# Steps and transfers of the first third of a fused attention and feed-forward kernel in another order

## The chip, the core and the metric

The kernel runs on one core of a Trainium2 chip. The metric is the device time of one launch in microseconds. Below, PE is TensorE, DVE is VectorE, ACT is ScalarE, POOL is GpSimd and SP is SyncE, which here issues nearly all transfers.

## What is computed

A gated linear attention over 768 positions (4 batches, 8 heads, head width 48) whose output, with the heads side by side, goes through a feed-forward block of width 2048 on 3072 tokens:

```python
def _attn_ref(q, k, v, f_logit) -> np.ndarray:
    B, H, S, D = q.shape
    f = 1.0 / (1.0 + np.exp(-f_logit))
    state = np.zeros((B, H, D, D), dtype=np.float32)
    y = np.zeros_like(q)
    for t in range(S):
        state = f[:, :, t, :, None] * state + np.einsum('bhd,bhe->bhde', k[:, :, t], v[:, :, t])
        y[:, :, t] = np.einsum('bhd,bhde->bhe', q[:, :, t], state)
    return y.astype(np.float32)
...
def _moe_ref(x, w_in, w_out) -> np.ndarray:
    h = x @ w_in
    relu6 = np.clip(h + 3.0, 0.0, 6.0)
    g = h * relu6 / 6.0
    return (g @ w_out).astype(np.float32)
```

## The kernel before

The 768 positions are cut into 6 chunks of 128. A chunk of one batch is a unit, so there are 24 units; unit i belongs to chunk i // 4. The four units of a chunk give one group of 512 tokens for the feed-forward block. The hidden width is cut into 16 blocks of 128, so a group has 16 block steps, and a step is numbered 16 * group + block.

What a unit i does, with the engine and the line of its instruction:

- `load` L371 (the gate logits, SP), `loadq` L378 (q and k, 512 KB, SP), `loadv` L383 (v, SP).
- `gate` L388 (sigmoid, ACT), `back` L395 and `fwd` L419 (the running products of the gates backward and forward, scans on DVE), `rend` L411 and `end` L414, `kmul` L408 and `qmul` L424 (k and q times these products, on DVE or POOL), `decay` L427.
- `tk` L482 (k turned, PE) and `ktok` L489 (its copy, ACT), `kv` L501 (k times v, PE), `carry0` and `carry1` L514 to L523 (the state), `att` L463 (q times k, PE), `mask` L470 (DVE), `qs` L533 and `av` L550 (the two parts of the output, PE).
- `xh` L569, `ym` L573 and `xl` L580 or L582 split the output into a high and a low part for the feed-forward block; `hole` L588 are two transfers of 48 KB that fill the rows which heads of 48 leave open.

What is done to each of the 16 weight blocks, once: `ld` L280 (its 64-bit form, 768 KB, SP), `lim` L290 or L292, `z` L298, `mid` L305, `dif` L310, `top` L314 (it is made a float again on ACT and DVE), `high` L326 (ACT) and `low`, `lowi`, `lowo` L329 (high and low part, DVE or POOL), for blocks 0 to 2 also `wd` L333 (a transfer).

What a block step does: `mm1` L619 (9 matmuls of 512 columns), `relu` L629 (ACT), `g` L633 (DVE), `gh` L642 (ACT), `gl` L646 (DVE or POOL), `mm2` L669 (9 matmuls). Blocks 0 to 2 of the first group are done in halves of 256 tokens, first the two units that come first (`mm1a` L691, `relua` L700, `ga` L705, `mm2a` L710), then the other two (`mm1b`, `relub`, `gb`, `mm2b`, on the same lines). `warm` L1007 and `tiny` L1014 are matmuls on a blank tile, of 512 and of 32 columns, whose results nobody reads.

Nothing schedules this on the chip. A list of 1518 words, ORDER, names every step once, as `step.number`, with the PSUM banks to use as a third part. The loop over ORDER writes the steps out in this order, and each engine works off its own instructions in the order in which they were written:

```python
            if ins.engine in ordered:
                after(ins, ordered[ins.engine])
```

Between engines there are semaphores for true dependencies and for buffers that are used again. All transfers of SP stand in one row, so that one which waits for its buffer holds those behind it. q and k have three buffers in turn, v three, the gates and their products two, PSUM two pairs of banks (0 and 1, 2 and 3) and a single one (4). Which steps run on POOL and on ACT is set by two more lists.

Of the kernel before, what the change touches and what calls it, by code (L numbers as in the profile page):

```python
# [60 lines left out]
mask.2 xl.1 ktok.2 rend.3 kmul.3 dif.1 lim.2 hole.1 wd.0 loadv.4 tk.3.0 fwd.3 kv.2.3 ktok.3 carry0.2 mid.2 z.2 kv.3.0
qmul.3 load.5 qs.2.2 top.1 carry1.3 end.3 carry1.2 att.3.0 dif.2 av.2 high.1 wd.1 ld.3 loadq.5 lowi.0 mm1a.0.4
carry0.3 top.2 gate.4 xh.2 mask.3 high.2 ym.2 qs.3.0 lowi.1 back.4 relua.0 xl.2 av.3 hole.2 mm1a.1.3 xh.3 lowi.2 end.4
ga.0 xl.3 mm2a.0 rend.4 relua.1 gate.5 lim.3 hole.3 ld.4 kmul.4 fwd.4 z.3 mm1a.2.0 ga.1 decay.4 qmul.4 back.5 mid.3
ld.5 tk.4.4 wd.2 mm2a.1 dif.3 ktok.4 ld.6 loadq.6 top.3 load.6 att.4.2 ld.7 kv.4.2 loadv.5 relua.2 ga.2 mask.4
carry0.4 carry1.4 high.3 low.3 lim.4 mid.4 ld.8 mm1b.0.4 ld.9 ld.14 mm1b.2.1 relub.0 z.4 dif.4 ld.10 end.5 loadv.7
lim.5 mm1b.1.0 rend.5 gb.0 relub.1 kmul.5 decay.5 mm1.3.2 top.4 mm2b.0 gb.1 high.4 mid.5 dif.5 z.5 low.4 mm2a.2 lim.6
top.5 mm2b.1 relub.2 mid.6 z.6 fwd.5 mm1.4.4 relu.3 dif.6 high.5 gb.2 g.3 gate.6 qs.4.0 qmul.5 low.5 tk.5.2 av.4
back.6 ktok.5 mm2b.2 loadv.6 xh.4 load.7 top.6 loadq.7 end.6 relu.4 ld.11 kv.5.2 ld.15 g.4 att.5.2 high.6 xl.4 mm1.5.4
gh.3 kmul.6 lim.7 lim.8 low.6 gh.4 gl.3 mm2.3 relu.5 rend.6 carry0.5 z.7 mask.5 carry1.5 z.8 gl.4 mid.7 mm2.4 g.5  # L70
decay.6 dif.7 gh.5 top.7 z.9 mm1.6.4 mid.8 high.7 gl.5 lim.9 dif.8 low.7 mm1.7.3 relu.6 top.8 mid.9 high.8 fwd.6
qs.5.0 relu.7 tk.6.2 av.5 dif.9 lim.10 g.7 mm2.5 loadv.8 xh.5 ld.13 g.6 hole.4 ktok.6 qmul.6 low.8 z.10 mm1.8.4 top.9
ld.12 gate.7 loadq.8 gh.6 back.7 high.9 att.6.2 gh.7 mid.10 gl.6 kv.6.0 lim.11 rend.7 mm2.6 xl.5 z.11 mask.6 kmul.7
dif.10 low.9 tk.7.2 mm1.9.3 ktok.7 top.10 relu.8 fwd.7 high.10 end.7 relu.9 gl.7 mm2.7 g.8 carry0.6 gh.8 g.9 low.10
mm1.10.4 carry1.6 gh.9 qmul.7 lim.12 mid.11 load.9 gl.8 mm2.8 z.12 hole.5 decay.7 dif.11 mid.12 dif.12 qs.6.2 top.11
att.7.0 loadq.9 av.6 load.8 top.12 kv.7.0 high.11 relu.10 gl.9 mm2.9 xh.6 carry0.7 mask.7 z.14 g.10 qs.7.0 xl.6 av.7
low.11 lim.13 z.13 hole.6 mm1.11.2 mid.13 lim.14 xh.7 loadv.9 gh.10 dif.13 high.12 mid.14 gl.10 mm2.10 relu.11 top.13
gate.8 g.11 low.12 mm1.12.3 gh.11 high.13 carry1.7 xl.7 gl.11 mm2.11 hole.7 relu.12 low.13 z.15 dif.14 loadq.10 gate.9
top.14 mm1.13.4 back.8 high.14 low.14 mm1.14.1 relu.13 g.13 g.12 gh.13 mm1.16.0 kmul.8 lim.15 gl.13 mid.15 dif.15
tk.8.2 top.15 mm2.13 back.9 high.15 end.8 gh.12 low.15 mm1.15.4 relu.14 rend.8 gl.12 fwd.8 mm2.12 relu.15 relu.16  # L80
qmul.8 ktok.8 g.14 load.10 att.8.2 g.15 gh.14 kv.8.2 g.16 mm1.17.4 mask.8 rend.9 gl.14 fwd.9 mm2.14 gate.10 gh.15
qmul.9 gl.15 mm2.15 lowo.0 back.10 mm1.19.1 outs.0 outv.1 end.9 gh.16 outs.2 kmul.9 gl.16 relu.17 mm1.18.0 od.2
load.11 rend.10 relu.19 g.17 od.0 decay.8 carry0.8 fwd.10 mm2.16 relu.18 g.19 end.10 carry1.8 g.18 tk.9.3 qmul.10
load.12 mm1.20.4 loadv.10 ktok.9 od.1 gh.17 kmul.10 lowo.1 gh.18 gate.11 decay.9 gl.17 qs.8.0 att.9.2 loadq.11 av.8
kv.9.2 xh.8 carry0.9 mm2.17 gate.12 carry1.9 mask.9 decay.10 lowo.2 back.11 mm1.21.2 gl.18 end.11 gh.19 gl.19 xl.8
tk.10.3 relu.21 mm2.18 ktok.10 g.21 relu.20 rend.11 back.12 qs.9.0 gh.21 fwd.11 att.10.2 loadq.12 av.9 kv.10.0 qmul.11
mm2.19 g.20 load.13 loadv.11 carry0.10 gl.21 loadv.12 carry1.10 rend.12 mm1.22.4 fwd.12 mask.10 mm2.21 relu.22 g.22
kmul.12 decay.11 gh.22 kmul.11 mm1.23.3 gate.13 qmul.12 xh.9 back.13 load.14 hole.8 relu.23 gl.22 mm2.22 xl.9 g.23
hole.9 tk.11.4 qs.10.0 ktok.11 att.11.2 gh.20 loadq.13 av.10 gate.14 gl.20 kv.11.0 loadv.13 tk.12.4 rend.13 mm2.20
ktok.12 gh.23 end.12 gl.23 mask.11 mm1.24.4 decay.12 kmul.13 mm1.25.3 mm2.23 relu.25 relu.24 g.25 g.24 mm1.29.3 gh.24  # L90
gl.24 fwd.13 mm1.26.4 relu.29 gh.25 xh.10 qmul.13 gl.25 mm2.25 load.15 xl.10 relu.26 carry0.11 back.14 mm2.24 g.29
g.26 qs.11.0 gh.26 att.12.2 gl.26 av.11 kv.12.2 xh.11 loadv.14 mm2.26 hole.10 gh.29 carry1.11 mask.12 gate.15
carry0.12 loadq.14 carry1.12 rend.14 mm1.27.4 tk.13.2 relu.27 mm1.30.3 g.27 gl.29 xl.11 mm2.29 relu.30 hole.11 gh.27
g.30 end.13 kmul.14 mm1.28.1 gl.27 gh.30 ktok.13 gl.30 decay.13 back.15 tk.14.0 mm2.30 fwd.14 mm1.31.2 qmul.14 load.16
mm1.32.4 relu.31 relu.28 g.31 end.14 g.28 mm2.27 relu.32 ktok.14 qs.12.0 gh.28 att.13.2 gh.31 loadq.15 gl.28 av.12
g.32 kv.13.2 xh.12 mm2.28 decay.14 gate.16 mask.13 rend.15 carry0.13 carry1.13 fwd.15 mm1.33.4 xl.12 qs.13.2 qmul.15
gl.31 load.17 att.14.0 loadv.15 av.13 kv.14.0 xh.13 mm2.31 relu.33 xl.13 kmul.15 back.16 hole.13 tk.15.2 g.33 end.16
loadq.16 mm1.35.3 ktok.15 hole.12 carry0.14 outv.4 gh.32 end.15 outs.3 gl.32 loadv.16 gate.17 rend.16 mm1.36.2 gh.33
decay.15 fwd.16 outs.5 relu.35 mm2.32 g.35 carry1.14 qmul.16 gl.33 load.18 mm1.34.4 kmul.16 gh.35 back.17 mm2.33
# [1058 lines left out]
```

## Time and profile before

| | |
|---|---|
| median of 3 runs | 460.57 us (460.49 to 461.0) |
| span of the profiled execution, first to last instruction | 458.9 us |
| PE busy | 448.2 us, 98% |
| DVE busy | 329.8 us, 72% |
| ACT busy | 225.9 us, 49% |
| POOL busy | 95.0 us, 21% |
| transfers | 44.95 MB, 98 GB/s over the span |

The profiled execution has no time of its own beside its span. The median of the runs is 1.7 us more than the span; this lies before the first and after the last instruction. A busy share is a mean over stages: in the first 110 us DVE is as busy as PE, and the transfers are busy in the first 60 us alone. Times inside the trace are counted from the first instruction.

### The profile page before, as it was taken

The page shows a single profiled execution, that of the slowest core. Times are in us where ns is not written, and L with a number is a line of the kernel's source. Part 1 is how long each engine was busy: PE and PEld are TensorE (multiplying, and loading weights), DVE is VectorE, ACT ScalarE, POOL GpSimd, SP SyncE. Part 2 cuts the span into 40 slices and gives each one's busy share as a digit, 9 for nine tenths or more (in the row PEclk, how much of TensorE's full clock was granted, in tenths as well). Part 3 has the DMA queues.
Part 4 walks back from the last instruction along what each step waited for, and adds up shares of the span by engine and source line. Part 5 has one row for each costly group of instructions (what it writes and reads, how often), then busy time and mean ns, then how long its engine had stood idle before and what let it go on. Part 6 is the DMA issues. An engine that isn't in the chain of part 4 may idle for free.

```text
span 458.9 us, 11919 instructions
## 1 busy us (share of the span) xinstructions
PE 448.2 (98%) x5092; PEld 387.8 (85%) x5092; DVE 329.8 (72%) x538; ACT 225.9 (49%) x390; POOL 95.0 (21%) x110
## 2 busy tenths in 40 slices
...
PEclk9999999999999999999999999999999999999999
...
GB/s 308 270 273 367 413 213 150 99 54 25 182 107 107 23 82 72 123 93 110 84 1 0 102 71 142 62 60 1 70 75 14 14 1 1 23 49 0 1 1 75
DMA packets 19116, 44.95 MB, mean 98 GB/s; under 512 B 2544, under 2 KB 8816, under 8 KB 19056
## 3 DMA queue, kind: packets, MB, share of 16 engines
...
q8 instruction: 42, 0.69, 0.6%
...
q14 instruction: 18, 0.15, 0.1%
...
## 4 chain that ended last, share of the span: by engine, by line
PE 90%; DMA 3%; DVE 3%; issue 1%; ACT 1%; SPq 1%; DVEq 0%; ACTq 0%
PE o L669 33%; PE pair L619 28%; PE single L619 11%; DMA raw<-w 3%; PE pair L533 3%; PE o L833 3%; PE pair L550 2%; PE pair L463 2%; PE single L833 2%; PE pair L833 2%; PE pair L501 2%; PE pair L482 1%; ACT workings L290 0%; DVE workings L314 0%; PE single L482 0%
## 5 line engine op out<-in xcount | busy, mean ns | idle before, releaser
L669 PE MATMUL o<-gg,weight 128*128 128x512 f32 x633 | 148.7, 382 | 0.3 <-issue 0.3
L619 PE MATMUL pair<-xts,weight 128*128 128x512 f32 x594 | 137.6, 381 | 0.0
L669 PEld LDWEIGHTS o<-gg,weight 128*128 128x128 f32 x633 | 117.6, 189 | 16.5 <-issue 0.2
L619 PEld LDWEIGHTS pair<-xts,weight 128*128 128x128 f32 x594 | 110.6, 189 | 15.5 <-DVE tg L633 0.3
L646 DVE TENSOR_TENSOR gg<-tg,gg 128x512 fp32r<-128x512 f32 x76 | 56.2, 746 | 34.4 <-ACT gg L642 34.0
L633 DVE SCALAR_TENSOR_TENSOR tg<-tg,pair 128x512 f32<-128x512 f32 x66 | 44.9, 682 | 41.3 <-ACT tg L629 40.9
L629 ACT ACTIVATE tg<-pair,half 128x512 f32<-128x512 f32 x66 | 44.9, 684 | 59.4 <-PE pair L619 56.7
L642 ACT ACTIVATE gg<-tg 128x512 fp32r<-128x512 f32 x79 | 48.8, 626 | 48.6 <-PE o L669 37.8
L619 PE MATMUL single<-xts,weight 128*128 128x512 f32 x243 | 57.9, 383 | 0.0
L619 PEld LDWEIGHTS single<-xts,weight 128*128 128x128 f32 x243 | 45.2, 189 | 6.6 <-ACT weight L326 0.3
L629 ACT ACTIVATE tg<-single,half 128x512 f32<-128x512 f32 x27 | 18.5, 686 | 31.0 <-PE single L619 28.8
L395 DVE TENSOR_TENSOR_SCAN scans<-scans,ones 112x516 f32<-112x516 f32 (+1 forms) x25 | 30.6, 1229 | 3.8 <-ACT scans L388 3.6
L408 POOL TENSOR_TENSOR qkf<-qkf,scans 112x512 f32<-112x512 f32 x14 | 20.4, 1455 | 59.2 <-DMA qkf<-unit 34.5
L424 POOL TENSOR_TENSOR qkf<-qkf,scans 112x512 f32<-112x512 f32 x11 | 15.8, 1439 | 70.4 <-DVE scans L419 48.7
L419 DVE TENSOR_TENSOR_SCAN scans<-scans,ones 112x516 f32<-112x516 f32 x24 | 29.8, 1240 | 0.4
L569 ACT ACTIVATE xts<-pair 112x512 fp32r<-112x512 f32 x24 | 14.3, 597 | 26.9 <-PE pair L550 22.7
L427 POOL TENSOR_TENSOR carried<-states,ends 112x192 f32<-112x192 f32 x12 | 9.0, 754 | 81.7 <-PE pair L533 48.1
L633 DVE SCALAR_TENSOR_TENSOR tg<-tg,single 128x512 f32<-128x512 f32 x27 | 18.4, 681 | 9.4 <-ACT tg L629 9.4
L470 DVE TENSOR_TENSOR a<-pair,causal 128x512 f32<-128x512 f32 x24 | 16.4, 681 | 8.1 <-PE pair L501 5.3
L582 DVE TENSOR_TENSOR xts<-pair,xts 112x512 fp32r<-112x512 f32 x22 | 15.0, 681 | 8.9 <-ACT xts L569 8.9
L757 POOL TENSOR_TENSOR temporary<-weight 128x256 f32<-128x256 f32 x14 | 10.7, 786 | 44.0 <-DVE tg L633 44.0
L800 ACT ACTIVATE ts<-ts 128x512 fp32r<-128x512 f32 x24 | 14.8, 627 | 9.9 <-DVE ts L796 8.6
...
## 6 DMA issues: line engine op xcount, KB each, us to landing
...
xts<-xts SPq DMA_DIRECT2D x48, 48.0 KB, 2.4
...
```

The source lines that it names most:

```text
L395: nc.vector.tensor_tensor_scan(flat(sf[:, p])[:, ::-1], gt[:, columns(p)][:, ::-1], flat(unit[:, p])[:, ::-1], 0.0, op0=ALU.mult, op1=ALU.add,
L408: engine("kmul", i).tensor_tensor(parts_of(t, 1), parts_of(t, 1), split(sf[:, :, 1:C + 1]), op=ALU.mult)
L419: nc.vector.tensor_tensor_scan(past, past, flat(rend), 0.0, op0=ALU.mult, op1=ALU.add)
L424: engine("qmul", i).tensor_tensor(parts_of(t, 0), parts_of(t, 0), split(to), op=ALU.mult)
L470: nc.vector.tensor_tensor(d["a"].rearrange("r p e t -> r e p t"), d["at"], causal.unsqueeze(1).unsqueeze(1).broadcast_to([128, 2, NP, HC]) ...
L619: nc.tensor.matmul(h, win(f, a, k), turned(g["xt"][:, k, :g["n"] // C, b]), start=i == 0, stop=i == 3 * KT - 1,)
L629: nc.scalar.activation(d["t"], d["h"], AF.Relu, bias=half, scale=1.0 / 6.0)
L633: nc.vector.scalar_tensor_tensor(d["t"], d["t"], 1.0, d["h"], op0=ALU.min, op1=ALU.mult)
L642: nc.scalar.activation(d["gg"][:, 0], d["t"], AF.Copy)
L646: engine("gl", g["first"] + f).tensor_tensor(d["gg"][:, 1], d["t"], d["gg"][:, 0].bitcast(F32), op=ALU.subtract)
L669: nc.tensor.matmul(g["o"][m], wout(f, a, m), halves_of(g[f]["gg"][:, b]), start=i == 0 and first_in(g, m), stop=f == NF - 1 and i == 2, sk ...
L833: nc.tensor.matmul(place[:, part * 256:(part + 1) * 256], left(a), halves_of(right(b)), start=i == 0 and first_in(g, bank_of), stop=False, ...
```

## The change

The first 718 of the 1518 words of ORDER, up to about block step 36 of 96 and unit 16 of 24, stand in another order. They are the same words, with the same banks; nothing else in the file differs, and the rest of ORDER is the same. The first two lines of the table, before and now:

```diff
-load.0 warm.2 loadq.0 warm.7 tiny.60 load.1 loadv.0 loadv.1 loadq.1 ld.0 gate.0 ld.1 back.0 rend.0 kmul.0 gate.1 fwd.0
-end.0 tk.0.2 tiny.12.3 qmul.0 ktok.0 back.1 load.2 kv.0.0 loadq.2 att.0.0 rend.1 warm.2 warm.1 mask.0 lim.0 kmul.1
...
+load.0 warm.2 warm.7 tiny.60 gate.0 warm.2 loadq.0 load.1 loadv.0 back.0 rend.0 kmul.0 loadq.1 ld.0 gate.1 tiny.12.3
+fwd.0 ld.1 loadv.1 tk.0.2 ktok.0 back.1 kv.0.0 carry1.0 qmul.0 rend.1 end.0 load.2 loadq.2 warm.1 carry0.0 fwd.1
```

The transfers that SP issues from the load of unit 3's gates on, before. `raw` is a weight block's 64-bit form (`ld`), `xts` a pair of `hole` transfers, `weight<-workings` is `wd`:

```order
L371 DMA scans_76<-unit 128x517
L378 DMA qkf3_311<-unit 128x1024
L280 DMA raw2_331<-w 128x3072
L588 DMA xts_105<-xts_105 16x3x256 x2
L383 DMA v2_410<-unit 128x400
L383 DMA v3_412<-unit 128x400
L371 DMA scans_76<-unit 128x517
L378 DMA qkf4_450<-unit 128x1024
L588 DMA xts_105<-xts_105 16x3x256 x2
L333 DMA weight0_392<-workings_106 128x384
```

The same place now:

```order
L371 DMA scans_76<-unit 128x517
L280 DMA raw2_285<-w 128x3072
L378 DMA qkf3_336<-unit 128x1024
L280 DMA raw3_361<-w 128x3072
L383 DMA v2_385<-unit 128x400
L383 DMA v3_411<-unit 128x400
L588 DMA xts_105<-xts_105 16x3x256 x2
L371 DMA scans_76<-unit 128x517
L378 DMA qkf4_460<-unit 128x1024
L333 DMA weight0_359<-workings_106 128x384
L588 DMA xts_105<-xts_105 16x3x256 x2
```

Block 2 stands one place ahead of unit 3's q and k, block 3 has come up from a place behind unit 5's gates to one ahead of both `hole` pairs, and `wd.0` stands ahead of the second pair. Further on `ld.4` has come ahead of the pairs of units 2 and 3.

DVE around block 3's `dif` and unit 5's `back`, before: `qmul.4`, `back.5`, `mid.3`, `dif.3`, `top.3`, `ga.2`.

```order
L424 TENSOR_TENSOR qkf4_450<-qkf4_450,scans_76 112x512
L395 SCALAR_TENSOR_TENSOR scans_76<-scans_76,ones_77 112x516
L305 TENSOR_SCALAR workings_106<-workings_106 128x768
L310 TENSOR_TENSOR workings_106<-workings_106 128x768
L314 SCALAR_TENSOR_TENSOR workings_106<-workings_106 128x768
L705 SCALAR_TENSOR_TENSOR th0_2_737<-th0_2_737,pair0_73 128x256
```

The same place now: `mid.3`, `qmul.4`, `decay.4`, `dif.3`, `back.5`, `top.3`, `mask.4`.

```order
L305 TENSOR_SCALAR workings_106<-workings_106 128x768
L424 TENSOR_TENSOR qkf4_460<-qkf4_460,scans_76 112x512
L427 TENSOR_TENSOR carried_97<-states_102,ends_104 112x4x48
L310 TENSOR_TENSOR workings_106<-workings_106 128x768
L395 SCALAR_TENSOR_TENSOR scans_76<-scans_76,ones_77 112x516
L314 SCALAR_TENSOR_TENSOR workings_106<-workings_106 128x768
L470 TENSOR_TENSOR a4_735<-pair1_74,causal_87 128x2x4x64
```

`dif.3` is now ahead of `back.5`; POOL's `kmul.5` waits for `back.5`.

DVE up to `g.3`, before: `top.5`, `mid.6`, `fwd.5`, `dif.6`, `gb.2`, `g.3`.

```order
L314 SCALAR_TENSOR_TENSOR workings_106<-workings_106 128x768
L305 TENSOR_SCALAR workings_106<-workings_106 128x768
L419 SCALAR_TENSOR_TENSOR scans_76<-scans_76,ones_77 112x516
L310 TENSOR_TENSOR workings_106<-workings_106 128x768
L705 SCALAR_TENSOR_TENSOR th1_2_826<-th1_2_826,pair0_73 128x256
L633 SCALAR_TENSOR_TENSOR tg0_3_840<-tg0_3_840,pair1_74 128x512
```

The same place now: `top.5`, `fwd.5`, `low.4`, `mid.6`, `gb.2`, `g.3`, `dif.6`.

```order
L314 SCALAR_TENSOR_TENSOR workings_106<-workings_106 128x768
L419 SCALAR_TENSOR_TENSOR scans_76<-scans_76,ones_77 112x516
L329 TENSOR_TENSOR weight4_823<-workings_106,weight4_823 128x768
L305 TENSOR_SCALAR workings_106<-workings_106 128x768
L705 SCALAR_TENSOR_TENSOR th1_2_821<-th1_2_821,pair0_73 128x256
L633 SCALAR_TENSOR_TENSOR tg0_3_841<-tg0_3_841,pair1_74 128x512
L310 TENSOR_TENSOR workings_106<-workings_106 128x768
```

`dif.6` has gone behind `g.3`; `low.4` stood ahead of `top.5` and is now behind `fwd.5`. On PE `tk.5`, which writes the banks that `g.3` reads, is the first of the steps behind `mm1.4` now; `qs.4`, which waits for `gb.2`, was first before.

## Rows read from the trace of the kernel before

**Rows 1.** The page: clock granted to PE in 40 slices, tenths of full speed.

```profile
PEclk9999999999999999999999999999999999999999
```

**Rows 2.** Windows: stretch, length, busy us of each engine (instructions), clock, DMA share, GB/s.

```profile
13.00:17.00 4.00, 3.54 (x104) 2.29 (x102) 3.70 (x6) 3.26 (x8) 0.00 (x0) 1.00 0.58 168
17.00:27.00 10.00, 8.61 (x306) 6.46 (x305) 9.38 (x16) 8.13 (x18) 1.19 (x1) 1.00 0.85 292
32.00:36.00 4.00, 3.98 (x55) 3.33 (x53) 3.96 (x7) 2.65 (x5) 0.63 (x1) 1.00 0.56 141
36.00:50.00 14.00, 13.53 (x137) 11.37 (x141) 13.26 (x23) 10.94 (x16) 3.19 (x3) 1.00 1.02 405
50.00:110.00 60.00, 59.91 (x721) 50.93 (x722) 58.56 (x94) 45.30 (x65) 16.91 (x11) 1.00 0.43 153
110.00:400.00 290.00, 289.62 (x3193) 253.36 (x3192) 185.64 (x298) 119.92 (x218) 60.70 (x69) 1.00 0.20 63
```

**Rows 3.** Chain that ended last, 31 to 50 us: start, us, what.

```profile
33.46 5.93 DMA raw<-w
...
48.75 0.65 PE pair L533 x28
```

**Rows 4.** Timeline of PE: start, us, instruction, count, idle before it.

```profile
30.09 1.27 PE L691 MATMUL pair<-xts,weight 128*128 128x256 f32 x9
31.20 1.46 PE L710 MATMUL o<-th,weight 128*128 128x256 f32 x6
...
49.39 0.57 PE L482 MATMUL pair<-ident,qkf 112*128 112x112 f32 x4
...
60.84 2.11 PE L619 MATMUL pair<-xts,weight 128*128 128x512 f32 x9
```

**Rows 5.** Timeline of DVE, the same columns.

```profile
10.69 1.42 DVE L419 TENSOR_TENSOR_SCAN scans<-scans,ones 112x516 f32<-112x516 f32 x1
...
21.55 0.69 DVE L470 TENSOR_TENSOR a<-pair,causal 128x512 f32<-128x512 f32 x1 [0.49 <-PE pair L463]
...
28.04 0.69 DVE L470 TENSOR_TENSOR a<-pair,causal 128x512 f32<-128x512 f32 x1
...
35.52 1.45 DVE L310 TENSOR_TENSOR workings<-workings 128x768 int16<-128x768 uint16 x1
...
43.44 0.42 DVE L705 SCALAR_TENSOR_TENSOR th<-th,pair 128x256 f32<-128x256 f32 x1 [0.33 <-ACT th L700]
...
47.82 0.54 DVE L310 TENSOR_TENSOR workings<-workings 128x768 int16<-128x768 uint16 x1
48.27 0.42 DVE L705 SCALAR_TENSOR_TENSOR th<-th,pair 128x256 f32<-128x256 f32 x1
48.60 0.69 DVE L633 SCALAR_TENSOR_TENSOR tg<-tg,pair 128x512 f32<-128x512 f32 x1
...
60.66 0.96 DVE L329 TENSOR_TENSOR weight<-workings,weight 128x768 fp32r<-128x768 f32 x1
```

**Rows 6.** Timeline of POOL, the same columns.

```profile
9.82 1.19 POOL L408 TENSOR_TENSOR qkf<-qkf,scans 112x512 f32<-112x512 f32 x1 [6.78 <-DMA qkf<-unit]
...
35.37 1.18 POOL L408 TENSOR_TENSOR qkf<-qkf,scans 112x512 f32<-112x512 f32 x1 [3.79 <-DVE scans L395]
...
121.82 1.00 POOL L329 TENSOR_TENSOR weight<-weight 128x384 fp32r<-128x384 f32 x1
```

**Rows 7.** Timeline of SP's issues.

```profile
14.95 0.33 SPq L378 DMA_DIRECT2D qkf<-unit  x1
15.33 0.42 SPq L280 DMA_DIRECT2D raw<-w  x1
...
22.86 1.20 SPq L588 DMA_DIRECT2D xts<-xts  x2
```

**Rows 8.** DMA issues, 22.8 to 24.1 us: count, KB each, median us to landing.

```profile
xts<-xts SPq DMA_DIRECT2D x2, 48.0 KB, 3.9
```

**Rows 9.** Timeline of PE's weight loads at 27 us.

```profile
27.24 0.41 PEld L691 LDWEIGHTS single<-xts,weight 128*128 128x128 f32 x3 [0.33 <-DMA xts<-xts]
```

More of the change, by code (lines that the diff above doesn't have):

```diff
@@ L55 @@
 ORDER = """
-load.0 warm.2 loadq.0 warm.7 tiny.60 load.1 loadv.0 loadv.1 loadq.1 ld.0 gate.0 ld.1 back.0 rend.0 kmul.0 gate.1 fwd.0
-end.0 tk.0.2 tiny.12.3 qmul.0 ktok.0 back.1 load.2 kv.0.0 loadq.2 att.0.0 rend.1 warm.2 warm.1 mask.0 lim.0 kmul.1
-fwd.1 tk.1.4 warm.2 z.0 warm.9 qmul.1 ktok.1 mid.0 load.3 carry1.0 dif.0 carry0.0 gate.2 top.0 qs.0.1 end.1 loadq.3
-av.0 back.2 ld.2 warm.1 xh.0 kv.1.3 lim.1 rend.2 fwd.2 ym.0 att.1.2 warm.5 end.2 xl.0 carry1.1 kmul.2 hole.0 carry0.1
-high.0 qmul.2 tk.2.4 qs.1.1 gate.3 mask.1 loadv.2 loadv.3 mid.1 av.1 back.3 att.2.2 load.4 loadq.4 xh.1 warm.3 z.1
@@ L61 @@
[L61 to L99, printed above, removed]
+load.0 warm.2 warm.7 tiny.60 gate.0 warm.2 loadq.0 load.1 loadv.0 back.0 rend.0 kmul.0 loadq.1 ld.0 gate.1 tiny.12.3
@@ new lines @@
+fwd.0 ld.1 loadv.1 tk.0.2 ktok.0 back.1 kv.0.0 carry1.0 qmul.0 rend.1 end.0 load.2 loadq.2 warm.1 carry0.0 fwd.1
+att.0.0 qmul.1 z.0 lim.0 mask.0 warm.2 kmul.1 mid.0 dif.0 load.3 ld.2 warm.9 tk.1.4 warm.1 ktok.1 kv.1.3 gate.2 qs.0.1
+loadq.3 top.0 carry0.1 lim.1 av.0 xh.0 high.0 ld.3 end.1 att.1.2 back.2 ym.0 rend.2 gate.3 loadv.2 carry1.1 warm.5
+kmul.2 fwd.2 tk.2.4 mask.1 xl.0 qs.1.1 qmul.2 loadv.3 hole.0 att.2.2 back.3 lim.2 mid.1 load.4 av.1 z.1 xh.1 mask.2
+xl.1 warm.3 loadq.4 kmul.3 rend.3 dif.1 wd.0 fwd.3 ktok.2 mid.2 tk.3.0 end.2 hole.1 kv.2.3 ktok.3 kv.3.0 loadv.4
@@ new lines @@
+qmul.3 carry0.2 qs.2.2 load.5 top.1 z.2 dif.2 gate.4 end.3 loadq.5 lowi.0 av.2 xh.2 high.1 att.3.0 ym.2 carry1.2 wd.1
+mm1a.0.4 carry0.3 top.2 mask.3 high.2 qs.3.0 av.3 back.4 xl.2 lowi.2 lowi.1 mm1a.1.3 ld.4 hole.2 relua.0 ga.0 kmul.4
+mm2a.0 xh.3 end.4 rend.4 xl.3 lim.3 relua.1 fwd.4 ga.1 tk.4.4 gate.5 z.3 mid.3 mm1a.2.0 hole.3 wd.2 qmul.4 ld.5
+decay.4 dif.3 ld.6 back.5 kmul.5 z.4 top.3 ktok.4 load.6 mm2a.1 att.4.2 carry1.3 kv.4.2 loadv.5 mask.4 carry0.4
+relua.2 ld.7 lim.4 ga.2 mid.4 loadq.6 carry1.4 ld.8 ld.14 high.3 dif.4 ld.10 mm1b.0.4 end.5 relub.0 low.3 mm1b.2.1
```

33 lines of the change are left out of this document (added).

## The prediction, made before the changed kernel was run

> **What bounds the kernel now.** I read the windows first, then the chain, then the timelines of PE, DVE and POOL. The windows [rows 2] split the span. From 50 us on PE is busy 59.91 of 60 us and then 289.62 of 290: whatever the change does, everything behind 50 us is a fixed row of PE work, and the time can fall only by as much as this row starts earlier and isn't interrupted. Ahead of it PE has idle time (0.46 us of 4 in 13 to 17, 1.39 of 10 in 17 to 27, 0.47 of 14 in 36 to 50), and more that is hidden in late matmuls. DVE is the other half: 9.38 of 10 us, 13.26 of 14, 58.56 of 60. Up to 110 us two engines are full, and one order has to please both. The transfers are full from 36 to 50 (share 1.02), yet have holes before: 0.58 in 13 to 17, 0.56 in 32 to 36 [rows 2]. The chain [rows 3] tells what set PE's pace: a weight block took 5.93 us from its issue at 33.46, then work goes over ACT and DVE to PE's `qs.4` at 48.75, which had waited for `gb.2` (48.27 to 48.69 on DVE). Right behind it `tk.5` at 49.39 [rows 4] starts 0.10 after `g.3` ends (48.60 + 0.69 = 49.29) [rows 5]. So PE's last wait ahead of its full stretch is for `g.3` on DVE, and I cost the change on DVE's list up to `g.3`, then on the list up to `low.7`, which PE needs next with little to spare: `low.7` ends at 61.62 [rows 5], and `mm1.7` (from 60.84 [rows 4]) needs it for its last third, near 62.1: 0.5 us. The clock is full in all slices [rows 1]; no gap of PE before cost it a slice, and the number of blank matmuls stays.
>
> **The change part by part.** No step is added or removed, so the work of each engine is the same; only waits move.
>
> *1. DVE, head.* `back.1` stands ahead of `qmul.0` now. It can't start before 8.07 (it waits for unit 1's sigmoid, not moved), so DVE idles some 0.7 us that `qmul.0` filled before; in return the 0.56 us wait of `mask.0` goes. But POOL's `kmul.1` (9.82, 1.19 us [rows 6]) will run behind `qmul.0`, until about 11.1, and `fwd.1` comes just then. The row for this is in the trace: `fwd.1` at 10.69 took 1.42 us [rows 5] and ended 1.10 after `kmul.1` (11.01), the same scan else takes 1.23. So `fwd.1` ends near 12.2, `qmul.1` 12.8, `mask.0` 13.4: weight block 0 (`mid.0`, 12.75 before) starts 0.6 later. From there to `mask.3` DVE took 15.3 us (to 28.04 [rows 5]). In it lie a 0.49 us wait for `att.2` [rows 5], which is ahead of `av.1` on PE now, 0.14 for unit 3's sigmoid, which ACT now does earlier, and hops of 0.1 where a step stands right behind the one it needs, four or five fewer now: 1.05 less. `mask.3` starts near 27.6, 0.45 earlier.
>
> *2. `dif.3`.* It took 1.45 us at 35.52 [rows 5]; the other fifteen take 0.53 to 0.56, as `dif.6` does (0.54). It ended 0.41 after POOL's `kmul.5` (35.37 + 1.18 = 36.55 [rows 6]). DVE stood still behind POOL for 0.9 us. Now `dif.3` stands ahead of `back.5`, and `kmul.5` waits for `back.5`: it can't be hit. `kmul.5` runs beside `top.3` and `mask.4` instead; `mask` reads PSUM, and a mask beside a `kmul` (10.08, beside 9.82) took its usual 0.69. Gain 0.9, cover for POOL 1.5 us against its 1.2.
>
> [...]
>
> *3. DVE from `mask.3` to the end of `g.3`.* Before: 28.04 to 49.29, 21.25 us. The steps at the pitch from start to start that each kind shows when nothing holds it: 4 scans of 1.14, 3 `top` of 0.92, 2 `low` of 0.87 and `lowi.2` 0.45, 3 `dif` of 0.48, 4 `mid` of 0.27, 6 `ga`/`gb` of 0.33, 5 of 0.60 (`qmul`, `mask`, `xl`, `g`), 3 of 0.27 (`decay`, `carry`), 2 `rend` of 0.1: 18.0 us. `dif.6` makes 0.5 more; the rest, 2.75, is waits: 0.98 `dif.3`, 0.33 for `relub.1` [rows 5], 0.2 a scan behind `lowi.1`, some 1.2 in hops and small waits for ACT. `dif.6` stands behind `g.3` now. So `g.3` ends at 27.6 + 18.0 + waits. The waits are 1.77 if all but `dif.3`'s stay and 0 at best; I take 0.6, nearer to the low end, since the steps that followed right behind what they need (`rend.4`/`fwd.4`, `mid.3`/`dif.3`, the two `carry`) now have others between, and since weight blocks 3 to 6 land well ahead (part 4), which frees ACT from its waits. `g.3` ends at 46.2, 3.1 earlier. PE can be there: from `mm1a.0` (27.27) to `tk.5` (49.39) its list is 18.0 us at its own pitch (nine matmuls of 256 columns 1.11, from 30.09 to 31.20 [rows 4]), so 45.3, if `mm1a.0` doesn't come later.
>
> *4. Transfers.* `ld.2` was issued at 15.33, behind `loadq.3` at 14.95, which waits for `qs.0` [rows 7]. It stands ahead now and fills the hole at 13 to 17. `ld.3` (768 KB) and `wd.0` (192 KB) now stand ahead of the second `hole` pair, for which PE waits at 27.24 [rows 9] (issued from 22.86, 3.9 us to landing [rows 7, 8]). At 405 GB/s [rows 2] the 960 KB are 2.4 us; the idle share before was 0.42 x 4 + 0.15 x 10 = 3.2 us. The pair lands between 24.4 and 29.6; with most of the holes filled and the pair issued some 0.5 earlier I take 27.0, no change for PE. `ld.4`, on the chain before, no longer waits for the pairs of units 2 and 3.
>
> *5. What is late next.* Up to `low.7` DVE has the same steps as before, so `dif.6` is paid after all: 3.1 - 0.5 = 2.6 earlier at `low.7`, and PE waits for it. Behind it the lists stay as tight as before. `lowo.2` (1.00 us on POOL [rows 6]) is moved from 122 us, where DVE had time, to behind `low.11`, near 84, beside two `dif`; up to 1.0. PE's blocks of small matmuls change places too. I take 0.4 for all that.
>
> **The sum.** 3.1 - 0.5 - 0.4 = 2.2. Span 458.9 - 2.2 = 456.7, and 1.7 outside the span to the median: 458.4.
>
> **The rivals.** *Same.* All waits of part 3 but `dif.3`'s stay (1.77, not 0.6: 1.2 less), and a step stands still behind `lowo.2` (1.0 instead of 0.4 within it, 0.6 more): 0.4 is left, 460.2. For it: two full engines, where a wait removed is soon found elsewhere. Against: DVE's waits before are few and known by row, and 0.9 of them can't come back at that place. [...]
>
> *More.* No wait on DVE in part 3, none new later, and PE takes up its 0.5 us before `low.7`: 2.2 + 0.6 + 0.4 = 3.2, or 457.4.
>
> *Slower.* The holes of the transfers aren't filled, and the second `hole` pair lands at 29.6. `mm1a.0` then starts 2.4 late, and PE needs 18.0 us and the waits it had (22.1 - 18.0 = 4.1, less 1.0 for `dif.3`): `tk.5` at 50.7 instead of 49.4, so 1.3 slower, 461.9. It decides from a landing later than 28.3. For it: a pair took 3.9 us to land behind less than is ahead of it now. Against: SP stood for `loadq.3` while the transfers idled.
>
> *The change does nothing* needs the same order on the engines; the lists differ from unit 0 on, so no chance of its own.
>
> **How the numbers follow.** Forecast (457.7 to 459.6) 0.52, more 0.13, same 0.23, slower 0.12. Faster by over 0.2% (0.9 us, about what can be told from no change) 0.65, within 0.23, slower 0.12. The range goes from 457.2, below the case with more, to 460.7, past the same; it leaves out the slower case and part of the ends.
>
> **What would show it.** `dif.3` at 0.55 us; `g.3` ending at 46 to 47 and `tk.5` right behind it; the second `hole` pair landing by 28 and the DMA share of 13 to 17 above 0.8; `mm1.7` 2 us or more earlier; PE 99.8% busy from then to 110. Wrong would be: a landing after 28.3, `dif` or scans of over 1.4 us at new places, or PE idle of 0.5 us and more between 50 and 110.

## The result, and the profile after

| | before | after |
|---|---|---|
| median | 460.53 us (459.16 to 461.0, 4 runs) | 465.47 us (463.46 to 466.59, 4 runs) |
| span of the profiled execution | 458.9 us | 464.9 us |

The ratio is 1.0108, 95% interval 1.008 to 1.0136: the new order is 5 us slower, where 2.2 us faster was forecast, and it lies outside the range. Run a second time beside later experiments it took 465.12 us, ratio 1.0099 (1.007 to 1.0127).

The front went much as forecast. The windows of after, columns as in [rows 2]: the hole of the transfers at 13 to 17 is filled (share 0.99, before 0.58). From 50 us on, where PE could lose nothing before, 1.95 us of 60 are idle, and 3.25 of 290. The last two lines are new stretches.

```profile
13.00:17.00 4.00, 3.13 (x135) 2.42 (x134) 3.31 (x6) 3.27 (x6) 0.00 (x0) 1.00 0.99 340
36.00:50.00 14.00, 13.89 (x167) 12.19 (x170) 13.07 (x25) 10.97 (x19) 4.57 (x4) 1.00 1.02 411
50.00:110.00 60.00, 58.05 (x667) 48.12 (x658) 58.79 (x90) 43.15 (x62) 18.65 (x12) 1.00 0.38 133
110.00:400.00 290.00, 286.75 (x3160) 249.48 (x3159) 181.81 (x291) 116.49 (x212) 53.40 (x61) 0.99 0.21 64
62.00:92.00 30.00, 28.05 (x422) 22.73 (x422) 29.77 (x47) 22.71 (x33) 9.33 (x6) 1.00 0.26 81
192.00:196.00 4.00, 4.00 (x15) 3.21 (x14) 2.60 (x6) 0.39 (x2) 0.00 (x0) 0.58 0.27 55
```

The page's clock line, 40 slices of the span. One isn't full, that of 186 to 198 us; before, all were [rows 1].

```profile
PEclk9999999999999999899999999999999999999999
```

PE's timeline of after, columns as in [rows 4]. `tk.5` comes 2.45 us earlier than in [rows 4], `mm1.7` 2.33 earlier (58.51, 60.84). Then three losses show. `mm1.11` waits 0.78 at 85.19, and by `mm1.12` (89.48, before 89.32) the lead is gone. `mm2.22` waits 0.81 for ACT. And in the middle of `av.13`, PE stands still 2.09 us with nothing that it waits for ("issue"); `mm2.31` behind it takes 3.71 us instead of 2.1, at a granted clock of 0.58 over 192 to 196 (last line of the windows), 0.50 over 191.94 to 195.35.

```profile
46.94 0.57 PE L482 MATMUL pair<-ident,qkf 112*128 112x112 f32 x4
...
58.51 0.70 PE L619 MATMUL pair<-xts,weight 128*128 128x512 f32 x2
...
85.19 2.18 PE L619 MATMUL pair<-xts,weight 128*128 128x512 f32 x9 [0.78 <-ACT xts L569]
...
89.48 2.11 PE L619 MATMUL pair<-xts,weight 128*128 128x512 f32 x9
...
140.04 1.13 PE L669 MATMUL o<-gg,weight 128*128 128x512 f32 x4 [0.81 <-ACT gg L642]
...
188.46 0.51 PE L550 MATMUL pair<-a,v 64*48 64x64 f32 x22
191.05 0.42 PE L550 MATMUL pair<-a,v 64*48 64x64 f32 x10 [2.09 <-issue]
191.40 3.71 PE L669 MATMUL o<-gg,weight 128*128 128x512 f32 x9
```

DVE's timeline of after, columns as in [rows 5]: `fwd.1`, `mask.3`, `dif.3`, `g.3`, then between 62 and 92 us `mid.9`, `dif.10`, `mid.11` and `lim.13`. `dif.3` takes 0.55 (before 1.45), and `g.3` ends at 46.83 (before 49.29). But `mid.11` takes 1.45 us, where a `mid` takes 0.35 (67.65).

```profile
9.06 2.01 DVE L419 TENSOR_TENSOR_SCAN scans<-scans,ones 112x516 f32<-112x516 f32 x1
...
27.59 0.69 DVE L470 TENSOR_TENSOR a<-pair,causal 128x512 f32<-128x512 f32 x1 [0.21 <-ACT carried L514]
...
33.56 0.55 DVE L310 TENSOR_TENSOR workings<-workings 128x768 int16<-128x768 uint16 x1
...
46.15 0.68 DVE L633 SCALAR_TENSOR_TENSOR tg<-tg,pair 128x512 f32<-128x512 f32 x1
...
63.12 0.76 DVE L305 TENSOR_SCALAR workings<-workings 128x768 uint16<-128x768 uint16 x1
...
67.65 0.35 DVE L305 TENSOR_SCALAR workings<-workings 128x768 uint16<-128x768 uint16 x1
67.92 0.68 DVE L470 TENSOR_TENSOR a<-pair,causal 128x512 f32<-128x512 f32 x1
68.52 0.95 DVE L310 TENSOR_TENSOR workings<-workings 128x768 int16<-128x768 uint16 x1
...
73.59 1.45 DVE L305 TENSOR_SCALAR workings<-workings 128x768 uint16<-128x768 uint16 x1
...
82.86 1.58 DVE L292 TENSOR_SCALAR workings<-raw 128x768 int16<-128x768 int16 x1
```

POOL's timeline of the same stretch tells why: `qmul.6`, `kmul.7`, `low.10`, `low.11`. The first ends at 63.67, and `mid.9` ends 0.21 later (63.88); the others end at 69.06, 74.83 and 84.03, and `dif.10`, `mid.11` and `lim.13` end 0.41, 0.21 and 0.41 later. It is the pattern of `dif.3` in the kernel before, four times.

```profile
61.84 1.83 POOL L424 TENSOR_TENSOR qkf<-qkf,scans 112x512 f32<-112x512 f32 x1 [6.20 <-DVE scans L419]
67.38 1.68 POOL L408 TENSOR_TENSOR qkf<-qkf,scans 112x512 f32<-112x512 f32 x1 [3.71 <-PE pair L501]
73.00 1.83 POOL L329 TENSOR_TENSOR weight<-workings,weight 128x768 fp32r<-128x768 f32 x1 [3.94 <-ACT weight L326]
81.97 2.06 POOL L329 TENSOR_TENSOR weight<-workings,weight 128x768 fp32r<-128x768 f32 x1 [7.14 <-ACT weight L326]
```

### The profile page after: what moved, and what is told of

Read it like the earlier page. It is cut to its first block, busy times and chain, and to the rows that moved or that the text cites. A ratio compares the mean times of both kernels' runs of the same rounds, so it can differ in the third digit from the quotient of the medians.

```text
span 464.9 us, 11925 instructions
## 1 busy us (share of the span) xinstructions
PE 449.3 (97%) x5092; PEld 387.3 (83%) x5092; DVE 331.5 (71%) x538; ACT 226.2 (49%) x390; POOL 94.2 (20%) x110
## 4 chain that ended last, share of the span: by engine, by line
PE 76%; DVE 12%; DMA 3%; issue 3%; ACT 3%; SPq 1%; POOL 0%; DVEq 0%; ACTq 0%
PE o L669 28%; PE pair L619 25%; PE single L619 9%; PE o L833 3%; DMA scans<-unit 2%; PE pair L533 2%; DVE workings L314 2%; PE single L833 2%; PE pair L833 2%; PE pair L550 2%; PE pair L463 2%; DVE tg L633 1%; DMA raw<-w 1%; DVE scans L419 1%; DVE workings L310 1%
## 5 line engine op out<-in xcount | busy, mean ns | idle before, releaser
L669 PE MATMUL o<-gg,weight 128*128 128x512 f32 x633 | 151.1, 386 | 1.3 <-ACT gg L642 0.8
L629 ACT ACTIVATE tg<-single,half 128x512 f32<-128x512 f32 x27 | 18.6, 690 | 36.9 <-PE single L619 31.9
L757 POOL TENSOR_TENSOR temporary<-weight 128x256 f32<-128x256 f32 x14 | 10.7, 784 | 44.0 <-DVE tg L633 44.0
```

The costliest lines, as they stand in the source:

```text
L629: nc.scalar.activation(d["t"], d["h"], AF.Relu, bias=half, scale=1.0 / 6.0)
L669: nc.tensor.matmul(g["o"][m], wout(f, a, m), halves_of(g[f]["gg"][:, b]), start=i == 0 and first_in(g, m), stop=f == NF - 1 and i == 2, sk ...
```

## The experiments

My theories were three: DVE held by POOL between 62 and 92 us; `mm1.23` ahead of `mm2.21`, by which `mm2.22` waits; the stop in `av.13`. The rival to the first was that up to 110 us any order of two full engines loses the same.

**Which third of the new order loses.** `e1_front_new` has the new order up to `mm1.7`, then the old one; `e2_new_to_165` is new up to `mm1.30`; `e3_old_to_110` old up to `mm1.17`, then new. One line at each seam, against before, before, and after:

```diff
-decay.6 dif.7 gh.5 top.7 z.9 mm1.6.4 mid.8 high.7 gl.5 lim.9 dif.8 low.7 mm1.7.3 relu.6 top.8 mid.9 high.8 fwd.6
+mm2.4 dif.7 top.7 high.7 lim.9 z.9 mid.8 gl.5 dif.8 mm1.6.4 low.7 kmul.6 mm1.7.3 relu.6 top.8 mid.9 high.8 fwd.6
...
+hole.10 carry1.12 mm1.30.3 gate.15 relu.27 tk.13.2 rend.14 loadv.14 g.27 gl.29 xl.11 mm2.29 relu.30 hole.11 gh.27 g.30
...
+qmul.8 ktok.8 g.14 load.10 att.8.2 g.15 gh.14 kv.8.2 g.16 mm1.17.4 lowo.2 decay.8 rend.9 gh.15 fwd.9 gl.14 relu.17
```

> The new order for every step that stood ahead of mm1.7 (62 us) before, the old order from there on. Theory: the front is faster as forecast (g.3 ended 2.5 us and mm1.7 started 2.3 us earlier in the changed kernel), and the whole loss comes later, from the new order behind 62 us. Then this kernel keeps most of the 2 us: 458.2 to 459.3 us, mm1.7 near 58.5, PE not stopped near 189 us. Rival: the old order behind 62 us can't use an earlier start, since DVE sets the pace there: 460.0 to 460.8. Rival: the new front disturbs the later part by itself, for instance by where the instruction fetches fall: above 461.5.

> The new order up to mm1.30 (165 us), the old order from there on. Theory: the changed kernel loses at two places, 2.0 us more than before in 62 to 90 us (DVE held by POOL) and 3.7 us more in 186 to 200 us (PE stands 2.1 us within av.13 and then runs at half clock for 3.4 us). Here the first loss stays and the second goes: 460.5 to 462.0 us, PE near 165 us about as late as before, no stop in 186 to 196. Rival: the stop comes from what lies ahead of it, and the old order meets it too: 464 to 466.

> The old order up to mm1.17 (107 us), the new order from there on. Theory: only the second loss is left, if the numbers of PE's instructions at the attention steps of 186 to 189 us are what matters: PE stands about 2 us within av.13, 463 to 465 us. Rival: the stop depends on how the front shifts PE against the transfers, and then it is gone or small here: 460 to 461.5.

Measured, beside 460.32 us for before: 460.01 us, ratio 0.9993 (0.9972 to 1.0014); 464.02 us, 1.006 (1.0039 to 1.008); 463.12 us, 1.0057 (1.003 to 1.0084). The front alone brings nothing that can be told: its `mm1.7` comes 1.24 us earlier than before's, and the old order behind it takes 0.99 longer to `mm2.22` (table below). So the loss of after has at least two places, which the table below parts: the order of 62 to 139 us and that behind 165. The runs of `e3_old_to_110` lie between 460.57 and 466.2, so what it has behind 165 isn't the same in every execution.

**The stop.** `e4_shift` is after with 32 of the blank matmuls at the start replaced by 4 longer ones; every later PE instruction has a number 56 lower.

```diff
-load.0 warm.2 warm.7 tiny.60 gate.0 warm.2 loadq.0 load.1 loadv.0 back.0 rend.0 kmul.0 loadq.1 ld.0 gate.1 tiny.12.3
+load.0 warm.2 warm.7 warm.4 tiny.28 gate.0 warm.2 loadq.0 load.1 loadv.0 back.0 rend.0 kmul.0 loadq.1 ld.0 gate.1 tiny.12.3
```

> The changed kernel with 32 of the 60 tiny blank matmuls replaced by 4 wide ones: the same PE time at the start (32 x 25 ns against 4 x 216 ns), but 56 PE instructions fewer ahead of everything. Theory: the 2.1 us stop within av.13 is a wait for instructions: 16 KB fetches bring 256 of them, the stop sits where a 256-piece ends, and the four attention steps of 187 to 189 us use up a piece faster than the next one comes. Moved by 56 instructions the end of the piece falls into the matmuls of mm2.31 and mm1.35, and the stop and the half clock behind it go: 461 to 462.5 us, PE clock 1.00 in all slices. Rival: the stop is a wait for data or a transfer that the profile doesn't name: it stays at the same instruction, 464.5 to 466.5.

Measured: 464.39 us, 1.0104 (1.0057 to 1.0151). In its timeline of PE `av.13` runs through:

```profile
189.45 0.63 PE L550 MATMUL pair<-a,v 64*48 64x64 f32 x32
190.01 2.21 PE L669 MATMUL o<-gg,weight 128*128 128x512 f32 x9
```

The stop went with the number, the waits between 62 and 139 us stayed, and another stop came up at the front (0.39 us in `kv.3`). The time missed the 461 to 462.5 of the theory all the same: the profiled run, 463.15, is the fastest of the four, and the slowest took 467.59. `e7_shift_late` does the same replacement in `e3_old_to_110`, and `e8_weave` moves one step in it, `mm2.31`, into the row of four attention steps:

```diff
-qmul.15 loadv.14 relu.33 loadv.15 kv.14.0 av.13 xh.13 xl.13 kmul.15 mm2.31 load.17 carry1.13 tk.15.2 mm1.35.3 g.33
+qmul.15 loadv.14 relu.33 loadv.15 mm2.31 kv.14.0 av.13 xh.13 xl.13 kmul.15 load.17 carry1.13 tk.15.2 mm1.35.3 g.33
```

> e3_old_to_110 (old order up to 110 us, new behind it; 463.1, runs from 460.6 to 466.2) with 32 of the 60 blank matmuls at the start replaced by 4 longer ones, so that every later TensorE instruction has a number 56 lower, at the same work. Theory (TensorE's 2.1 us stop inside av.13 is a wait for its own instructions, at the end of a piece of 256, and sits there by the number alone): no idle time over 0.5 us in 186 to 200 us, granted clock 1.0 there, all runs at 460.5 to 461.7, median 461.0 (the wait of 0.8 us at 137 us stays). Rival (the stop belongs to av.13, its data or its buffers): it stays at av.13 and the runs lie between 460.6 and 466 as before, median 463.

> e3_old_to_110 with one step moved: mm2.31 (1.94 us of TensorE with only 18 instructions, its inputs ready at 182.8 us) ahead of kv.14 instead of behind av.13, in the midst of the four attention steps att.14, qs.13, kv.14, av.13. Theory (these four use up 256 instructions in less time than the next piece takes to arrive): the piece has 1.9 us more, the stop of 2.1 us shrinks to 0.3 us or less, the clock stays at 1.0, median 460.8 to 461.3. Rival (the stop has another cause, which the order of two steps doesn't touch): a stop of 2 us remains in part of the runs, median 463, with half clock behind it.

Measured, beside 460.29 us: 465.52 us, 1.0125 (1.007 to 1.018), and 464.29 us, 1.0081 (1.0056 to 1.0105). Both were to be near 461, and both lost the stop in `av.13` as the theory said. In the timeline of PE of `e7_shift_late` the new numbers put a stop of 2.02 us into `kv.3` at the front, where the DMA share is 0.88 (23 to 25 us):

```profile
27.18 0.25 PE L501 MATMUL pair<-v,ktok 64*64 64x48 f32 x2 [2.02 <-issue]
```

In that of `e8_weave` PE waits 1.91 us for DVE ahead of `tk.15`. `mm2.31` had been the cover for `xl.13` and `carry1.13`, which `tk.15` needs. I had priced the stop and not the cover:

```profile
189.98 0.63 PE L550 MATMUL pair<-a,v 64*48 64x64 f32 x32
192.52 0.57 PE L482 MATMUL pair<-ident,qkf 112*128 112x112 f32 x4 [1.91 <-DVE states L523]
```

Behind that wait, too, PE ran at half clock (window of `e8_weave`, clock 0.50), here without a stop for instructions:

```profile
193.00:196.40 3.40, 3.40 (x10) 2.68 (x10) 2.89 (x5) 3.27 (x8) 0.91 (x1) 0.50 0.63 198
```

What the stops have in common I read from all traces. The page lists a queue of 42 packets with 0.69 MB, 16 KB each, which, as the numbers below show, carries PE's instructions:

```profile
q8 instruction: 42, 0.69, 0.6%
```

The number of an instruction counts all that PE's list holds up to it: matmuls, weight loads and the sequencer's own (semaphore waits and a few more). Seven of the stops:

| kernel | instruction of PE | packet, us | PE goes on | stood still |
|---|---|---|---|---|
| after | 5312 | 188.10 to 189.44 | 191.05 | 2.09 |
| e11_after_again | 5312 | 190.08 to 190.96 | 192.49 | 2.08 |
| e3_old_to_110 | 5312 | 188.00 to 189.28 | 190.66 | 1.81 |
| e10_stop_left | 5312 | 187.57 to 188.53 | 189.94 | 1.50 |
| e6_dif3 | 1216 | 27.95 to 28.83 | 30.38 | 1.62 |
| e7_shift_late | 960 | 24.42 to 25.62 | 27.18 | 2.02 |
| e5_port | 704 | 18.80 to 19.79 | 21.27 | 0.97 |

Counted so, 16 pauses of PE in the 13 traces, 0.36 to 2.3 us from one start to the next, end at the numbers 704, 960, 1216, 3520 or 5312, which all leave 192 when divided by 256 (give or take one where a matmul and its weight load start together); each pause of over 0.3 us that the timelines put down to "issue" is among them. PE goes on 1.30 to 1.61 us after the packet's end. So a packet brings the next 256 instructions (in after the 13th packet sets off 236 ahead of 3520 and the 20th 103 ahead of 5312: seven packets for 7 x 256), and where PE gets there first, it stands. In after the packet for 5312 set off with 103 instructions to go, 0.65 us of work, since `att.14`, `qs.13`, `kv.14` and `av.13` have 64 small instructions each, one such row every 0.5 us; in before the same packet set off with 250 to go. At the ends of most of the 40 pieces PE doesn't stand; in after it stands at this one for 2 us.

**DVE held by POOL.** `e5_port` is `e2_new_to_165` with five places set otherwise, so that what stands on DVE beside a POOL step is a step that reads PSUM: `g.7` ahead of `mid.9`, `mid.11` behind `carry1.6`, `xl.6` and `g.10` ahead of `lim.13`, `lowo.2` back at 122 us. Two of the lines:

```diff
-tk.6.2 hole.4 mm2.5 ld.13 relu.7 lim.10 g.6 gate.7 gh.6 ld.12 mid.9 dif.9 ktok.6 qmul.6 g.7 top.9 mm1.8.4 z.10 qs.5.0
+tk.6.2 hole.4 mm2.5 ld.13 relu.7 lim.10 g.6 gate.7 gh.6 ld.12 g.7 mid.9 dif.9 ktok.6 qmul.6 top.9 mm1.8.4 z.10 qs.5.0
...
-low.9 end.7 mm1.9.3 rend.7 gl.7 relu.8 top.10 high.10 fwd.7 g.8 mid.11 relu.9 xl.5 tk.7.2 carry0.6 ktok.7 low.10 mm2.7
+low.9 end.7 mm1.9.3 rend.7 gl.7 relu.8 top.10 high.10 fwd.7 g.8 relu.9 xl.5 tk.7.2 carry0.6 ktok.7 low.10 mm2.7
```

> The new order up to 165 us (as e2_new_to_165, 464.0), with five places set otherwise so that VectorE no longer stands still beside a POOL step: g.7 ahead of mid.9, mid.11 behind carry1.6, xl.6 and g.10 ahead of lim.13, lowo.2 back at 122 us. Theory (VectorE held by POOL between 62 and 92 us is what gave the front's lead away): mid.9 0.35 us instead of 0.76, mid.11 0.4 instead of 1.45, lim.13 0.8 instead of 1.6; TensorE's lost time of 62 to 92 us falls from about 4.0 to about 1.9 us, and the time to 461.5 to 462.5. Rival (up to 110 us two engines are full and any order of this kind loses about as much, elsewhere): the steps named get short, other waits come up in the same stretch, lost time 3.5 or more, 463.5 to 464.5.

Measured: 461.42 us, 1.0024 (1.0002 to 1.0047), 2.6 us less than `e2_new_to_165`. In DVE's timeline `mid.9`, `mid.11` and `lim.13` take 0.38, 0.34 and 0.55, and `g.7` and `g.10`, which read PSUM and stand beside POOL's `qmul.6` and `low.11` now, take 0.71 and 0.67, as a `g` does elsewhere:

```profile
66.38 0.71 DVE L633 SCALAR_TENSOR_TENSOR tg<-tg,pair 128x512 f32<-128x512 f32 x1
66.97 0.38 DVE L305 TENSOR_SCALAR workings<-workings 128x768 uint16<-128x768 uint16 x1
...
78.80 0.34 DVE L305 TENSOR_SCALAR workings<-workings 128x768 uint16<-128x768 uint16 x1
...
85.58 0.67 DVE L633 SCALAR_TENSOR_TENSOR tg<-tg,single 128x512 f32<-128x512 f32 x1
86.17 0.55 DVE L292 TENSOR_SCALAR workings<-raw 128x768 int16<-128x768 int16 x1
```

In the window of 62 to 92 us PE is busy 29.53 us instead of the 28.05 of after:

```profile
62.00:92.00 30.00, 29.53 (x435) 24.81 (x435) 29.71 (x49) 24.75 (x35) 7.20 (x4) 1.00 0.34 115
```

The theory holds, its rival falls. What the three steps had lost by POOL, 0.41, 1.10 and 1.03 us in after, is 2.5 together, near the 2.3 that the second column of the table below gets back. The moves also bring `g.7`, `xl.6` and `g.10` forward on DVE; what that is worth by itself isn't parted from it. `mid` and `lim` have one input each and were held all the same: `mid.11` took 1.45 us beside `low.10` in after and 0.34 in `e5_port`, where it stands beside no POOL step.

**`dif.3` alone.** `e6_dif3` is before with `ld.3` ahead of `wd.0`, and `mid.3` and `dif.3` ahead of `back.5`.

```diff
-ga.0 xl.3 mm2a.0 rend.4 relua.1 gate.5 lim.3 hole.3 ld.4 kmul.4 fwd.4 z.3 mm1a.2.0 ga.1 decay.4 qmul.4 back.5 mid.3
-ld.5 tk.4.4 wd.2 mm2a.1 dif.3 ktok.4 ld.6 loadq.6 top.3 load.6 att.4.2 ld.7 kv.4.2 loadv.5 relua.2 ga.2 mask.4
+ga.0 xl.3 mm2a.0 rend.4 relua.1 gate.5 lim.3 hole.3 ld.4 kmul.4 fwd.4 z.3 mm1a.2.0 ga.1 decay.4 qmul.4 mid.3 dif.3
+back.5 ld.5 tk.4.4 wd.2 mm2a.1 ktok.4 ld.6 loadq.6 top.3 load.6 att.4.2 ld.7 kv.4.2 loadv.5 relua.2 ga.2 mask.4
```

> The order of before with one thing of the change: ld.3 ahead of wd.0, and mid.3 and dif.3 ahead of back.5, so that kmul.5 on POOL can't hold dif.3. Both theories: dif.3 0.55 us instead of 1.45. Theory A (the old order behind 62 us doesn't keep a lead, as e1_front_new showed): g.3 some 0.5 to 0.9 earlier, mm1.12 as before within 0.3 us, time 460.0 to 460.5. Theory B (a small lead is kept where nothing else is moved): mm1.12 0.6 to 0.9 earlier, 459.4 to 459.8.

Measured: 461.35 us, 1.0007 (0.998 to 1.0034), runs from 458.15, the lowest of this study, to 463.42. Neither theory told of that width. In its trace `dif.3` takes 0.56 as it should, but in PE's timeline `qs.3` stops for 1.62 us, at instruction 1216:

```profile
30.38 0.45 PE L533 MATMUL pair<-qkf,carried 48*64 48x64 f32 x12 [1.62 <-issue]
```

In the window behind it the granted clock is 0.57; nine matmuls of 256 columns take 2.29 us there (31.51), where before took 1.27 (30.09):

```profile
31.30:35.30 4.00, 4.00 (x34) 3.62 (x26) 2.97 (x6) 2.16 (x5) 0.00 (x0) 0.57 0.29 87
```

The packet set off at 27.95 with 12 instructions to go; in before, with nearly the same order, at 25.97 with 150 to go. The gain of `dif.3` can't be read from this median: the stop of its profiled execution covers it.

**All mended but one.** `e9_mended` is `e5_port` with `g.22` ahead of `carry0.10`, `fwd.12` and `xl.9`; `e10_stop_left` is after with the same six moves, PE's list untouched; `e11_after_again` is after.

```diff
-kv.10.0 gh.21 mm2.19 loadv.11 loadv.12 gl.21 relu.20 g.20 mm1.22.4 relu.22 mask.10 mm1.23.3 xh.9 carry0.10 fwd.12 xl.9
-mm2.21 g.22 hole.9 gate.13 back.13 carry1.10 gh.22 gl.22 hole.8 qmul.12 load.14 mm2.22 relu.23 g.23 tk.11.4 decay.11
+kv.10.0 gh.21 mm2.19 loadv.11 loadv.12 gl.21 relu.20 g.20 mm1.22.4 relu.22 mask.10 mm1.23.3 xh.9 g.22 carry0.10 fwd.12
+xl.9 mm2.21 hole.9 gate.13 back.13 carry1.10 gh.22 gl.22 hole.8 qmul.12 load.14 mm2.22 relu.23 g.23 tk.11.4 decay.11
```

> e5_port (new order up to 165 us with the five places on VectorE and POOL set otherwise, 461.4) and one step more: g.22 ahead of carry0.10, fwd.12 and xl.9 on VectorE, which needs only relu.22, done at 136.1 us. Theory (the wait of 0.81 us at mm2.22 is for gh.22, which is late because g.22 stands behind a scan of 1.2 us and xl.9): that wait goes, 1.0 us, median 460.3 to 460.6; runs without a stop of TensorE ahead of 50 us at 459.3 to 460. Rival (TensorE waits there for something else as well, or VectorE is late with the next steps): a wait of 0.5 us or more in 136 to 146 us remains, 461.2 to 461.6.

> The whole new order (after, 465.5) with the same six moves on VectorE and POOL as e9_mended and nothing else; TensorE's list is after's. Theory (three causes that add up: VectorE held by POOL 2.5 us, g.22 1.0 us, and TensorE's stop at its instruction 5313 with half clock behind it): 462 to 462.5 in runs with the stop, and the difference to e9_mended, 1.5 to 2.5 us, is the stop alone; a stop of 1.8 to 2.3 us inside av.13 in the profile, 1.3 to 1.6 us from the end of the last 16 KB fetch to TensorE's next instruction. Rival (the tail of the new order costs nothing by itself): same time as e9_mended within 0.5 us.

> The changed kernel once more, unaltered, in the same company as the two mended ones. Theory: 464.5 to 466 median; the waits of VectorE behind POOL between 62 and 92 us (mid.9, mid.11, lim.13) and the one at mm2.22 as in the first profile within 0.1 us, since they follow from the order; the stop inside av.13 in most executions; mm1.7 anywhere between 58.5 and 61.5 us, by when the first transfers land. Rival (the first profile was a single one of its kind): no stop and a time of 462 or less.

Measured, beside 459.77 us: 460.52 us, 1.0008 (0.9985 to 1.003); 463.92 us, 1.0066 (1.0038 to 1.0095); 465.12 us, 1.0099 (1.007 to 1.0127). So 4.6 us of the slowdown are gone in `e9_mended`, which has the old order behind 165 us; 1.2 of them come with the six moves alone (`e10_stop_left`). In its timeline of PE `mm2.21` and `mm2.22` run as one row, with 0.29 us of a new wait near its end. `mm1.23` still stands ahead of `mm2.21` there, so that place costs little by itself:

```profile
137.32 3.40 PE L669 MATMUL o<-gg,weight 128*128 128x512 f32 x15
141.01 0.92 PE L669 MATMUL o<-gg,weight 128*128 128x512 f32 x3 [0.29 <-DVE gg L646]
```

`e10_stop_left` stops in `av.13` as after does (timeline of PE):

```profile
189.94 0.38 PE L550 MATMUL pair<-a,v 64*48 64x64 f32 x10 [1.50 <-issue]
```

And so does `e11_after_again`:

```profile
192.49 0.42 PE L550 MATMUL pair<-a,v 64*48 64x64 f32 x10 [2.08 <-issue]
```

The sizes for `e10_stop_left` were missed: 463.9 instead of 462 to 462.5, so 3.4 more than `e9_mended`, while its trace accounts for about 2; and 1.2 less than `e11_after_again`, while the second column of the table shows 3.2. Its runs go from 460.63 to 465.04, and five of eleven have a mean granted clock of 0.992 or 0.993 where the profiled one has 0.998: half clock in part of the runs is the likely rest, but no trace of such a run shows it.

## Why the prediction was wrong

Cut at three starts on PE, the profiled executions add up (all in us from the trace; the rest behind `mm1.36` is 266.8 to 267.4 in each):

| kernel | start to `mm1.7` | `mm1.7` to `mm2.22` | `mm2.22` to `mm1.36` |
|---|---|---|---|
| before | 60.84 | 78.16 | 52.93 |
| after | 58.51 | 81.53 | 57.43 |
| e11_after_again | 59.96 | 81.52 | 55.75 |
| e4_shift (new order, other numbers) | 59.57 | 81.47 | 53.36 |
| e2_new_to_165 | 61.99 | 81.52 | 53.09 |
| e5_port | 61.80 | 79.26 | 53.09 |
| e9_mended | 60.94 | 78.32 | 53.51 |
| e10_stop_left | 60.80 | 78.29 | 55.55 |
| e1_front_new | 59.60 | 79.15 | 52.94 |
| e3_old_to_110 (old front) | 60.92 | 79.01 | 57.16 |

**Part 1 (head), right by two errors.** `fwd.1` was held by `kmul.1` as forecast (2.01 us, to 1.09 after `kmul.1`'s end). But the load of unit 1's gates landed at 5.74, so `back.1` started 0.9 earlier than before, and `mid.0` at 12.32, not at 13.35. From there to `mask.3` DVE took 15.27, as before, not the 14.25 that I had worked out. `mask.3` at 27.59 hit the 27.6 by chance: in the other seven traces with the new front it starts at 27.4 to 31.3, in six of them behind the 28.04 of before.

**Part 2 (`dif.3`), right:** 0.55 or 0.56 in all eight traces with the new front and in `e6_dif3`.

**Part 3 (`mask.3` to `g.3`), right:** 18.6 forecast, 19.24 in after, 18.1 to 20.1 in the eight traces, 21.25 before.

**Part 4 (transfers), too early.** The second `hole` pair landed at 27.12 in after, as I took it (27.0), but at 27.5 to 30.3 in the other seven traces with the new front, and at 25.9 to 27.2 in five with the old one. Five of the eight are behind 28.3, from which my slower case decides. By the same traces `mm1.7` starts between 58.51 and 61.99, 60.4 in the mean: of a lead of 2.3 us some 0.4 is left over the executions. Of this slower case only its place was right: it takes the lead away and makes no 461.9 by itself (`e1_front_new`, 460.0). In three of the five (`e2_new_to_165`, `e5_port`, `e10_stop_left`) the pair was issued at 24.5 to 26.0, against 22.5 to 23.6 in the others, and ahead of that PE had lost time: 3.4 us at half clock from 10.7 on (11 blank matmuls took 3.67, in before 2.54), a stop of 0.97 with half clock behind it, a stop of 0.34. In the other two (`e4_shift`, `e9_mended`) it was issued in time and took 5.3 and 5.6 us to land, against 4.2 in after. What sets either is open.

**Part 5 (what is late next), the step that failed.** "Behind it the lists stay as tight as before" and 0.4 for the rest. The second column of the table has 81.5 in all four traces with the whole new order there, 3.4 more than before, to 0.1, where 0.4 was forecast for all that comes behind the front: `e5_port` takes 2.3 of it away and `g.22` 0.9. Behind the front I had priced DVE held by POOL at one step, `lowo.2` (up to 1.0). The order told on which DVE steps the others would fall. My sign for it, PE idle of 0.5 us or more between 50 and 110, showed. And "PE's blocks of small matmuls change places too" had no price of its own: the third column is 2.6 to 4.5 more wherever the stop at 5312 comes, and no rival had it. In the trace of before there was a gap of 0.36 us to be seen at 122.94, between two matmuls that wait for nothing, at number 3520, right behind such a packet; I left that queue out.

The sum for after: 2.33 gained, 3.37 and 4.50 lost, 0.4 behind `mm1.36`: 5.9, the difference of the spans to 0.1. Up to 165 us the order can be mended to the time of before (`e9_mended`), and no version here has a median that is told from before's on the fast side; only single runs of `e6_dif3` (458.15, 458.82) lie below all of before's.
